# Block records by plain loads on SyncE, and a small block's second product as four strips of 192 outputs

## The chip, the cores and the metric

The kernel runs on one core of one Trainium2 chip. The metric is the device time of one execution in microseconds (us); lower is better. Times of the kernel before are the median of three runs. Beside them one execution was profiled; it has its own time, and a span, from the first to the last instruction of the program.

## The reference

Sigmoid attention over 8 batches, 12 heads, 448 positions and a head size of 64 gives 3584 rows of 768 numbers. Each row then goes through a mixture of experts with a skip: a row whose skip score is not positive stays as it is, another goes through the one expert, out of eight, that its gate logits choose.

```python
scores = scale * np.matmul(q, k.transpose(0, 1, 3, 2)) - np.log(S)
attn = 1.0 / (1.0 + np.exp(-scores))
x = (attn @ v).transpose(0, 2, 1, 3).reshape(3584, 768)
do_compute = x @ w_skip > 0
e_idx = np.argmax(xc @ w_gate, axis=1)          # xc = x[do_compute]
h = np.maximum(xc[mask] @ w1[e], 0.0)           # 768 -> 1024
y[mask] = gate_w[mask, None] * (h @ w2[e])      # 1024 -> 768
out[do_compute] = xc + y
```

## The kernel before

The first part (to about 284 us) is the attention, over 48 pairs of heads; meanwhile each row is given its expert, and a record (gate weight, row number) is scattered into `lst`, a table in device memory with a stretch of rows for each expert. From 284 to 324 us two blocks of 128 rows of the most used expert are computed. Meanwhile VectorE works out the list of the remaining blocks: from per-expert sums (`gt`, 17 columns) and one-hot masks over 64 list places (`m_f`, `m_a`, `m_p`), small matmuls into `ptab` make two things. One is `rix`, for each of the 64 places a column of 128 row numbers of `lst`: VectorE forms the first row of each place (`row`, L1072 to L1074) and a matmul with `ones_f` spreads it over 128 partitions (L1077). The other is `slots`, three rows of numbers for each place (L1081): whether the weights of another expert are to be loaded, of which, and the kind of the block.

From 324 us a loop (L1537) runs over the remaining 14 blocks. All engines run the same loop: each reads the kind of the block from `slots` into a register (a TENSOR_LOAD, L1089), branches (L1526, L1527, L1532) and runs one of four arms:

- FULL and SPLIT (`block`): 128 rows with weights that were split into a high and a low part (`wh1`, `wl1`, `wh2`, `wl2`), three products for each. SPLIT also makes the split weights of the next expert from the raw ones.
- HALF (`half`): up to 64 rows, with raw weights (`raw1`, `raw2`).
- FEW (`few`), the small block: up to 32 rows, with raw weights. TensorE's columns work as four groups of 32. In the first product (L1391, `ph`) each group makes 128 hidden numbers at a time. In the second (L1391, `py`) group g makes 384 outputs over one half of the eight chunks of h; so two groups hold partial sums of the same outputs. ScalarE scales two of them into `yt` (L1444), and VectorE adds the other two, scaled (L1446).

In FEW and HALF, SyncE issues the eight loads of the next expert's raw weights, 768 KB each: four of w1 after the first product (L1213), four of w2 after the second (L1222), on SyncE's one queue.

Rows and records are fetched ahead. During a block, `fetch` on GpSimd copies the row numbers out of `rn` (the record after next, L1267), issues an indirect DMA for the rows `xn` (L564), and another for the next record `rn` from `lst` by a column of `rix` (L1115); the ops on `jk`, `rn` and `rx` (L1266, L1268, L1269) stand before it as waits. `shift` on VectorE (L1283) moves `rix` by one column each block, through `riv`. `take_rec` (L1322) takes the record at the next block. `put` on GpSimd copies the row numbers (L1287, L1288), waits for the two halves of `yt` (L1293), copies them into `ys` (L1302) and issues the scatter that adds them to `out` (L574).

The order of instructions on each engine is written by hand (`manual_schedule`), in the order of the program's text; a framework adds the semaphores. After the last iteration the program ends when the last scatter has landed.

## Time and profile before

| | us |
|---|---|
| median of three runs | 526.61 (526.55 to 526.98) |
| the profiled execution's own time | 526.53 |
| its span | 524.8 |
| granted TensorE clock | 0.995 |
| TensorE matmul busy | 508.7 (97%) |
| VectorE, ScalarE, GpSimd busy | 296.1, 281.0, 262.5 |
| attention, first two blocks, loop (from the chain of waits) | to 284, to 324, to the end |

In the span's last 200 us the fourteen blocks of the loop follow one another; five of them are FEW, at 403.8, 428.9, 454.3, 480.3 and 507.2 us, and the last one ends the program. The profile counts an engine as busy when it computes; branches, register loads and the issue of DMAs belong to the engine's sequencer, which is listed apart (PEq, SPq and so on). The chain of waits is followed back from the last instruction: each piece is either work or what released it.

### The profile page before, as it was taken

To read this page: it belongs to the slowest core of one execution; us is meant where nothing else is said; L and a number is where in the kernel's file an instruction comes from. 1 tells how busy PE (TensorE), PEld (TensorE's weight loads), DVE (VectorE), ACT (ScalarE), POOL (GpSimd) and SP (SyncE) were. 2 spreads that over 40 slices of the span, in tenths; PEclk is the share of its full clock that TensorE was granted. 3 is DMA by queue.
4 is the path that set the end of the run, shared out by engine and by line. 5 is a ranking of instruction groups with operands and counts; after the bars stand their busy time and mean duration, and the time that the engine had idled before them with its cause. 6 is when DMAs were issued, how large, how long until landed. Compare 5 with 4: busy or idle time off the path is not lost.

```text
span 524.8 us, 15310 instructions
## 1 busy us (share of the span) xinstructions
PE 508.7 (97%) x5033; PEld 339.2 (65%) x5034; DVE 296.1 (56%) x721; ACT 281.0 (54%) x485; POOL 262.5 (50%) x414
## 2 busy tenths in 40 slices
PE   8999999999999999999989999999999999999991
PEld 7765555545545456555445989948669797978790
DVE  4556757648667676687684962862222322269422
ACT  5776776767767668677664211942112323268322
POOL 4523553443557666766574332553333645455644
PEclk9999999999999999999999999999999999999997
DMA  8999787898999999999955023979393959695942
GB/s 211 209 257 200 150 187 156 178 175 173 195 206 234 220 203 221 196 204 213 199 105 114 11 92 105 389 210 347 99 364 119 317 230 310 240 328 227 346 184 47
DMA packets 140288, 107.21 MB, mean 204 GB/s; under 512 B 97099, under 2 KB 112731, under 8 KB 140240
## 3 DMA queue, kind: packets, MB, share of 16 engines
q1 hardware_dynamic: 134000, 97.66, 70.0%
q0 software_dynamic: 4576, 8.65, 6.9%
q8 instruction: 30, 0.49, 0.4%
q10 hardware_dynamic: 1664, 0.26, 0.3%
q14 instruction: 18, 0.15, 0.1%
HBM read 98.49 MB, written 17.56 MB: 221 GB/s over the span
## 4 chain that ended last, share of the span: by engine, by line
PE 89%; DVE 3%; SPq 2%; DMA 2%; issue 1%; ACT 1%; POOL 0%; POOLq 0%; ACTq 0%; DVEq 0%
PE s L212 23%; PE pa L240 21%; PE ph L516 11%; PE py L544 11%; PE b_ph L516 3%; PE b_py L544 3%; PE ph L1391 3%; PE py L1458 2%; PE ph L1458 2%; PE pxt L492 2%; PE py L1391 2%; PE pl L280 1%; PE pht L530 1%; DMA out_dram<-y 1%; SPq L263 1%
## 5 line engine op out<-in xcount | busy, mean ns | idle before, releaser
L232 ACT ACTIVATE at<-s,bias 128x896 f32<-128x896 f32 (+1 forms) x191 | 173.3, 913 | 82.1 <-PE s L212 71.2
L212 PE MATMUL s<-x 64*64 64x448 f32 (+1 forms) x1528 | 165.4, 498 | 1.3 <-DVE wh L485 0.9
L240 PE MATMUL pa<-at,v 64*64 64x448 f32 (+1 forms) x1536 | 163.0, 489 | 0.0
L176 POOL COPY kq<-kq 32x896 f32<-32x896 f32 (+1 forms) x96 | 88.1, 917 | 94.6 <-DMA kq<-in_q_dram 59.0
L212 PEld LDWEIGHTS s<-x 64*64 64x64 f32 x1528 | 80.0, 191 | 53.1 <-issue 28.6
L240 PEld LDWEIGHTS pa<-at,v 64*64 64x64 f32 x1536 | 62.5, 133 | 54.9 <-issue 47.8
L194 DVE STREAM_TRANSPOSE x<-kq 128x448 f32<-128x448 f32 x94 | 80.8, 934 | 5.0 <-POOL kq L176 5.0
L250 DVE TENSOR_TENSOR xt<-xt,pa 128x448 f32<-128x448 f32 x48 | 29.7, 620 | 54.4 <-ACT xt L673 49.6
L414 POOL DMA_INDIRECT lst<-rec,idx x32 | 31.7, 989 | 17.4 <-DVE xt L250 5.8
L486 POOL TENSOR_TENSOR wl<-wr,wh 128x384 fp32r<-128x384 f32 (+1 forms) x28 | 31.2, 1125 | 12.6 <-DVE wh L485 8.1
L255 DVE STREAM_TRANSPOSE y<-xt 128x448 f32<-128x448 f32 x48 | 31.0, 645 | 6.8 <-DMA out_dram<-y 5.2
L574 POOL DMA_INDIRECT out_dram<-ys,rp x15 | 23.7, 1580 | 16.6 <-issue 8.4
L525 ACT ACTIVATE hs<-ph 128x512 f32<-128x512 f32 x14 | 8.3, 596 | 43.9 <-PE ph L516 37.5
L536 DVE TENSOR_TENSOR hl<-pht,hh 128x512 fp32r<-128x512 f32 x14 | 9.7, 690 | 36.5 <-ACT hh L535 22.8
L544 PE MATMUL py<-wh,hh 128*128 128x384 f32 x112 | 29.8, 347 | 0.0
L502 DVE TENSOR_TENSOR xl<-pxt,xh 128x384 fp32r<-128x384 f32 x30 | 15.3, 552 | 25.3 <-ACT xf L1097 17.8
L544 PE MATMUL py<-wh,hl 128*128 128x384 f32 x112 | 28.8, 338 | 0.0
L544 PE MATMUL py<-wl,hh 128*128 128x384 f32 x112 | 28.7, 337 | 0.0
L516 PE MATMUL ph<-wh,xh 128*128 128x512 f32 x84 | 25.7, 402 | 1.1 <-ACT yt L1444 0.8
L516 PE MATMUL ph<-wl,xh 128*128 128x512 f32 x84 | 26.6, 403 | 0.0
L673 ACT ACTIVATE xt<-pa 128x448 f32<-128x448 f32 x48 | 25.7, 536 | 0.8 <-PE pa L240 0.8
L516 PE MATMUL ph<-wh,xl 128*128 128x512 f32 x84 | 24.5, 395 | 0.0
(277 smaller groups left out, 686.4 us busy)
## 6 DMA issues: line engine op xcount, KB each, us to landing
raw<-in_moe_w_dram SPq DMA_DIRECT2D x64, 768.0 KB
v<-in_v_dram SPq DMA_DIRECT2D x48, 256.0 KB
out_dram<-y SPq DMA_DIRECT2D x192, 56.0 KB
kq<-in_k_dram SPq DMA_DIRECT2D x46, 224.0 KB
kq<-in_q_dram SPq DMA_DIRECT2D x46, 224.0 KB
wr<-in_moe_w_dram SPq DMA_DIRECT2D x12, 256.0 KB
wr<-in_moe_w_dram SPq DMA_DIRECT2D x16, 192.0 KB
lst<-fill SPq DMA_DIRECT2D x4, 464.0 KB
```

The source lines that it names most:

```text
L176: nc.gpsimd.tensor_copy(a[BT:, :, :, :BT], a[:BT, :, :, BT:])
L194: nc.vector.transpose(xs[:, n].rearrange("p (r j) -> p j r", j=NJ), t.rearrange("p (j d) -> p j d", d=D)[:, :, :BT],)
L212: nc.tensor.matmul(sc[m * D : (m + 1) * D, j, : qs.stop - qs.start], xs[r, 0, first::NR7], xs[r, 1, qs], start=True, stop=True,)
L232: nc.scalar.activation(at[:, :, :n], sc[:, :, :n], AF.Sigmoid, bias=bias, scale=SCALE)
L240: nc.tensor.matmul(pa[j * D : (j + 1) * D, r, qs], vt[rs, j, r + c if c < 3 else 3 * (1 - r), :], at[rs, j, : qs.stop - qs.start], start=( ...
L250: nc.vector.tensor_tensor(x, x, pa[:, 1, :S], op=ALU.add)
L255: nc.vector.transpose(y, xts[b][:, hp, :])
L414: put = nc.gpsimd.indirect_dma_start(out=lst[:, :], out_offset=bass.IndirectOffsetOnAxis(ap=idx[:, c : c + 1], axis=0), in_=rec[:, c, :], ...
L486: nc.gpsimd.tensor_tensor(lo, r, hi, op=ALU.subtract)
L516: nc.tensor.matmul(ph[h], a[:, j * P : (j + 1) * P], w[j][h], start=(n == 0), stop=(n == len(t) - 1),)
L544: last = nc.tensor.matmul(half_y(py, o), a[h][:, js], w[j][:, o * H2 : (o + 1) * H2], start=(j == 0 and n == 0), stop=(j == NK2 - 1 and n ...
L1391: nc.tensor.matmul(dst[g * SM : (g + 1) * SM, :n], a, w, start=(j == 0), stop=(j == most - 1), tile_position=(0, g * SM),)
```

## The change

Two things are changed together. First, the records come by plain DMAs issued by SyncE. `slots` gets a fourth row, ROW, the first row in `lst` of each place's block; SyncE reads it into a register and loads 128 consecutive rows of `lst`. `rix`, `ones_f`, the three ops on `row`, the matmul L1077, `shift`, `riv`, `rx` and the waits for them in `fetch` go. Second, in FEW's second product each of the four groups makes a strip of 192 outputs over all eight chunks of h. No partial sums are left to add: ScalarE scales two strips into `yt`, VectorE the other two.

```diff
-    V.tensor_scalar(row, m_f, f_rf, None, op0=ALU.mult)
-    V.scalar_tensor_tensor(row, m_a, f_ra, row, op0=ALU.mult, op1=ALU.add)
-    V.scalar_tensor_tensor(row, m_p, f_rp, row, op0=ALU.mult, op1=ALU.add)
-
     gemm1(1, range(3), xh0, xl0, ph)
-    nc.tensor.matmul(ptab[:, :NS], ones_f, row, start=True, stop=True)
-
-    HAS, NXT, TYP = range(3)
-    for n, (j, m) in enumerate(((2, m_a), (7, m_p), (12, m_f))):
+
+    ROW, HAS, NXT, TYP = range(4)
+    for n, (j, m) in enumerate(((1, m_a), (6, m_p), (11, m_f))):
         nc.tensor.matmul(
...
-    V.tensor_scalar(rix, ptab[:, :NS], slot_q, None, op0=ALU.add)
-    slots = const.tile([3, NS], I32, name="slots")
+    slots = const.tile([4, NS], I32, name="slots")
...
-    def gather_rec(dst, idx):
-
-        nc.gpsimd.indirect_dma_start(
...
+    def load_rec(dst, col):
+        row = entry(ROW, col, SP, NE * CAP - P)
+        nc.sync.dma_start(dst, lst[ds(row, P), :])
 
     for j in range(2):
-        gather_rec(recs[:, j, :], rix[:, j + 2 : j + 3])
-    gather_rec(rn, rix[:, 4:5])
+        load_rec(recs[:, j, :], slice(j + 2, j + 3))
+    load_rec(rn, slice(4, 5))
...
-    skip(4616 - DM)
+    skip(4688 - DM)
...
-    def fetch():
+    def fetch(i):
 
         pool.tensor_tensor(xn[:, 0:1], xn[:, 0:1], zf, op=ALU.add)
-        pool.tensor_tensor(jk, rn[:, 0:2], rn[:, 0:2], op=ALU.add)
         pool.tensor_copy(ri, rn[:, 1:2])
-        pool.tensor_tensor(rn[:, 0:1], rn[:, 0:1], zf, op=ALU.add)
-        pool.tensor_tensor(rx, rix[:, 5:6], zero, op=ALU.add)
         pool.tensor_tensor(rp[1], ri, zero, op=ALU.add)
         pool.tensor_tensor(rq, rp[1], zero, op=ALU.add)
         got = gather(xn, rp[1])
...
-        gather_rec(rn, rx)
+        load_rec(rn, ds(i + 5, 1))
...
         ready_x()
-        shift(dve)
 
-        for n, j in enumerate((0, 2, 1, 3)):
+        Q2 = DM // 4
+        for n, m in enumerate((0, 2, 4, 6, 1, 3, 5, 7)):
             for g in range(4):
-                o, h = g // 2, g % 2
-                m = j + h * (NK2 // 2)
                 quarter(
-                    py[h],
+                    py[g // 2],
                     g,
-                    H2,
-                    ht4[:, j % 2, 2 * h + j // 2, :],
-                    raw2[m][:, o * H2 : (o + 1) * H2],
+                    Q2,
+                    ht4[:, m % 2, m // 2, :],
+                    raw2[m][:, g * Q2 : (g + 1) * Q2],
                     n,
-                    NK2 // 2,
+                    NK2,
                 )
         for g in range(4):
             load_w2(g, nx)
-        for m in range(2):
-            for o in range(2):
...
+        for g in range(4):
+            s = slice(g * Q2, (g + 1) * Q2)
+            p = py[g // 2][g * SM : (g + 1) * SM, :Q2]
+            if g < 2:
+                nc.scalar.activation(yt[:SM, s], p, AF.Copy, scale=recs[:SM, 0, 0:1])
+            else:
+                weigh_sum(yt[:SM, s], p, recs[:SM, 0, 0:1])
```

## The prediction

> **What bounds the kernel now.** I read the busy shares first, then the shares of the chain of waits, then the chain through the loop, then the sequencer's own instructions.

> ```profile
> PE 508.7 (97%) x5033; PEld 339.2 (65%) x5034; DVE 296.1 (56%) x721; ACT 281.0 (54%) x485; POOL 262.5 (50%) x414
> ...
> PE 89%; DVE 3%; SPq 2%; DMA 2%; issue 1%; ACT 1%; POOL 0%; POOLq 0%; ACTq 0%; DVEq 0%
> ```

> TensorE (PE) is busy for 97% of the span and is 89% of the chain. So an edit counts only where it changes what PE executes, or makes PE stand, or lies behind PE's last instruction. VectorE (DVE) and GpSimd (POOL) are busy for about half the time: work taken from them in mid-loop is worth nothing by itself. The next rows are the chain through one small block (FEW at 428.87) into the FULL block behind it (start, duration, engine, tile, line).

> ```profile
> 428.87 2.81 PE ph L1391 x96
> 431.69 0.26 PE pht L1412
> ...
> 432.71 2.75 PE py L1391 x32
> 435.47 0.28 issue
> 435.75 6.53 PE ph L516 x27
> ```

> The first product is 96 matmuls in 2.81 us, the second 32 in 2.75 us, and at 435.47 PE stands for 0.28 us in "issue", which is no engine and no transfer: PE's sequencer was not yet through with the branch to the next arm. That small gap is where the change can hurt, so I read the four ends of FEW blocks that have a block behind them.

> ```profile
> 410.34 6.49 PE ph L516 x27
> 488.70 6.49 PE ph L516 x27
> 461.75 0.47 PE L516 MATMUL ph<-wh,xh 128*128 128x512 f32 x1 [0.80 <-ACT yt L1444]
> ```

> ```profile
> L1537 PEldq COMPARE_BRANCH  x1: 239/239/239, 408.5 to 408.5; - x1
> L1537 PEldq COMPARE_BRANCH  x1: 237/237/237, 433.7 to 433.7; - x1
> L1537 PEldq COMPARE_BRANCH  x1: 239/239/239, 459.1 to 459.1; - x1
> L1537 PEldq COMPARE_BRANCH  x1: 237/237/237, 486.5 to 486.5; - x1
> L1089 PEldq TENSOR_LOAD <-slots x1: 459/459/459, 409.1 to 409.1; - x1
> L1089 PEldq TENSOR_LOAD <-slots x1: 972/972/972, 434.3 to 434.3; - x1
> L1089 PEldq TENSOR_LOAD <-slots x1: 1265/1265/1265, 459.7 to 459.7; - x1
> L1089 PEldq TENSOR_LOAD <-slots x1: 446/446/446, 487.1 to 487.1; - x1
> L1089 PEldq TENSOR_LOAD <-slots x13: 302/308/1265, 340.0 to 505.0; - x13
> L1412 PEldq FUSED_REGOPS  x1: 42/42/42, 430.9 to 430.9; - x1
> ```

> The loop's branch (L1537) runs on PE's sequencer while PE still has matmuls queued. It starts at 408.5, 433.7, 459.1 and 486.5; the products end at 410.34 and 488.70 (the next block follows at once), 435.47, and 461.75 - 0.80 = 460.95. So the sequencer's lead is 1.84, 1.77, 1.85 and 2.2 us. From the branch to the next block's first matmul it needs 2.05 us at 433.7 (to 435.75) and 2.65 us at 459.1 (to 461.75); at the other two at most its lead. Much of that is the read of the block's kind: 0.459, 0.972, 1.265 and 0.446 us behind a FEW, where the fastest of 13 took 0.302 and the median 0.308. So the stalls now are 0, 0.28, 0.80 and 0: 1.08 us.

> **The change part by part.** The sum is made against the profiled execution, 526.53 us with a span of 524.8, 0.08 below the median of 526.61.

> *Prologue.* The matmul that spread the row numbers goes; it lies on the chain:

> ```profile
> 309.29 0.40 PE ptab L1077 x2
> ```

> That is -0.4. Its neighbours are PE as well, so nothing takes its place; bounds -0.8 (if the products behind it were held by the shorter VectorE chain too) to 0 (if the later `slots` holds PE instead). The first records now come by SyncE, in front of the first w1 load on its queue, and not by three gathers on POOL: POOL's gather form costs about 1 us of POOL each (0.99 at L1115, below), so they should land no later. I cost it at nothing.

> *FEW's products.* Each of five FEW blocks makes 16 quadruples of 192 columns for 8 of 384. The rows above hold two sizes of the same form: 96 matmuls are 24 quadruples of 128 in 2.81 us, 117 ns each; 32 are 8 of 384 in 2.75 us, 344 ns each. The line through both gives 0.885 ns a column and 174 ns at 192: 16 are 2.78 us, +0.03 a block, +0.1 in all (bounds 0 and +0.5, the latter with a fixed cost three times as large).

> *The end of FEW.* This is the main cost. I take PE's queue to hold a number of instructions, not a time, and the second product becomes 64 matmuls of 2.78 / 64 = 43 ns in place of 32 of 86 ns. Now the branch at 433.7 has 1.77 us or 20 matmuls of 86 ns in front of it, fewer than the 27 found next, so the queue is not full there; with 64 matmuls it would be. How far ahead is the sequencer then? At 430.9 PE's sequencer ran the register operation behind the first product's last matmul (L1412), and that product ended at 431.68: 0.78 us, or 27 matmuls of 2.81 / 96 = 29 ns, each with its weight load, were outstanding. 27 matmuls of 43 ns are 1.17 us; the branch comes a few instructions behind the last matmul, for which I allow 0.12 (three of the 42 ns of that operation): the branch is 1.05 us ahead of the product's end, against 1.77 to 2.2 now. The stall is then the time from branch to first matmul less 1.05. With the reads as recorded the first and the last end need the 2.05 of the second with their own read in place of its, 2.05 - 0.97 + 0.46 = 1.54 and 1.53, so the stalls are 0.49 and 0.48; the second 2.05 - 1.05 = 1.00; the third 2.65 - 1.05 = 1.60. In all 3.57, which is 2.5 more than before. With every read at 0.302 the path is 1.38 (2.05 - 0.97 + 0.30), three times 0.33, and at the SPLIT (2.65 - 1.265 + 0.302 = 1.69) 0.64: 1.63, +0.55 more than before. Which read is right I can't see: they were slow only behind a FEW, when a busy stretch of DMA begins, and that stays about as it was, but no row shows the cause. I take +1.1, nearer the faster end because 9 of the 13 reads were fast and the reads now fall later against the start of the w2 loads.

> [...]

> *The tail.* The last block is a FEW; nothing runs behind its scatter, and the chain after its product is short enough to read (start, duration, engine, line):

> ```profile
> 514.00 1.17 ACT L1444 ACTIVATE yt<-py,recs 32x384 f32<-32x384 f32 x2 [0.73 <-DVE xl L502]
> 514.83 1.26 DVE L1446 SCALAR_TENSOR_TENSOR yt<-py,recs,yt 32x384 f32<-32x384 f32 x2
> 515.11 0.99 POOL L1115 DMA_INDIRECT rn<-lst,rx  x1 [0.31 <-issue]
> 516.12 0.20 POOL L1287 TENSOR_TENSOR rp<-rid,zero 128x1 int32<-128x1 int32 x1
> 516.54 0.18 POOL L1293 TENSOR_TENSOR jk<-yt 32x2 f32<-32x2 f32 x1
> ...
> 518.65 1.41 POOL L574 DMA_INDIRECT out_dram<-ys,rp  x1 [0.62 <-issue]
> ```

> ```profile
> 514.00:515.00 1.00, 0.00 (x0) 0.00 (x0) 0.86 (x4) 0.97 (x2) 0.80 (x1) 1.00 0.81 154
> 515.00:515.50 0.50, 0.00 (x0) 0.00 (x0) 0.47 (x2) 0.17 (x1) 0.39 (x1) 1.00 0.03 0
> ```

> ```profile
> L1446 DVE SCALAR_TENSOR_TENSOR yt<-py,recs,yt 32x384 f32<-32x384 f32 x10 | 6.1, 613 | 0.7 <-ACT yt L1444 0.4
> L1444 ACT ACTIVATE yt<-py,recs 32x384 f32<-32x384 f32 x10 | 5.7, 574 | 4.4 <-DVE xl L502 2.2 <-DVE riv L1283 1.3 <-PE py L1391 0.7
> L1408 ACT ACTIVATE hs<-ph 128x128 f32<-128x128 f32 x10 | 2.8, 278 | 33.5 <-PE ph L1391 31.9 <-PE pxt L492 1.7
> ```

> Now the two halves pass ScalarE and then VectorE and end at 516.09; POOL is behind the record's gather until 516.10, so the two are equally late, and POOL's put starts at 516.12. Both go. POOL's gather of `rn` (0.99, and 0.31 of issue) is gone, so POOL could start put near 514.8, but put's first copy also waits for the scatter before it: the DMA rows show 154 GB/s until 515 and nothing after, so 515.05. The strips: 192 columns on ScalarE, by the line through 128 (278 ns) and 384 (574), are 352 ns; two are 0.70. VectorE's two (384 take 613) are about 0.76, beside ScalarE's and behind nothing. From the product's end at about 514.0 `yt` is whole at about 514.9, plus the small queue effect of a later start. So put is set by 515.05, 1.07 before 516.12, and what follows (518.65 and the landing) moves with it: -1.0. Bounds: -1.7 (if the wait for the previous scatter isn't the limit and put follows `yt`), 0 (if a later product end and POOL's other work give all of it back).

> *Records in mid-loop.* The record of the block after next now goes through SyncE's queue, behind the w1 loads that a FEW has just issued. The rows are stretches of the second block's time: length, then busy time of PE, PE's loads, VectorE, ScalarE, POOL, clock, DMA share, GB/s.

> ```profile
> 433.00:436.00 3.00, 2.72 (x33) 1.28 (x26) 0.98 (x3) 2.13 (x10) 2.19 (x9) 1.00 0.63 163
> 436.00:439.00 3.00, 3.00 (x14) 2.41 (x14) 1.94 (x9) 0.82 (x2) 1.43 (x2) 1.00 1.04 258
> 439.00:446.00 7.00, 7.00 (x38) 5.86 (x37) 0.92 (x3) 1.79 (x3) 4.03 (x14) 1.00 1.04 395
> ```

> ```profile
> 444.09 0.16 DVE L1322 COPY recs<-rn 128x2 f32<-128x2 f32 x1
> 447.76 0.69 DVE L536 TENSOR_TENSOR hl<-pht,hh 128x512 fp32r<-128x512 f32 x1 [3.51 <-issue]
> 470.06 0.16 DVE L1322 COPY recs<-rn 128x2 f32<-128x2 f32 x1
> 470.13 3.90 DVE L1234 TENSOR_TENSOR wl<-raw,wh 128x512 fp32r<-128x512 f32 x6
> ```

> Four w1 loads are 3.1 MB: 0.49 and 0.77 by 439, the remaining 1.9 MB at 395 GB/s until about 444. The record then lands at about 445, VectorE takes it at 444.09 now, and its next work of weight is at 447.76, after 3.5 us of idleness: hidden. At the SPLIT it is tighter: the same pace from 454.3 puts the record at 470 to 472, it is taken at 470.06, and VectorE has 3.9 us of `wl` right behind, on which the next products of PE hang. 0 to +0.8; I take 0, since in VectorE's order only that copy and what stands behind it slips, and PE at that time is in products of older weights for several us.

> [...]

> The sum: -0.4 + 0.1 + 1.1 - 1.0 = -0.2, 526.3 for the profiled execution and 526.4 with the 0.08 to the median. No change that can be seen.

> **The rivals.**
> 1. Slower: the slow reads stay as recorded, 0.46 to 1.27 us behind each FEW. Then the third term is +2.5 and the time 526.4 + 1.4 = 527.8. For it: all four reads behind a FEW were slow in this trace; against: they differ by a factor of three from one another, so an earlier or later one may fall anywhere. It decides slower from about 2.4 us of added stalls.
> 2. Faster: the queue holds five matmuls more (if the operation at 430.9 itself came 0.15 us, five of 29 ns, behind the last issue) and the reads are fast. Leads are then 1.05 + 5 x 0.043 = 1.27 or, without the allowance, 1.39; stalls at 1.39 are 3 x 0 + (1.69 - 1.39) = 0.3, so -0.8 in place of +1.1: 526.4 - 1.9 = 524.5; with the second read as recorded, 0.67 more: 525.2. For it: nine of thirteen reads were fast. Against: it needs both.
> 3. Slower: the records are late where VectorE or POOL waits for them. At the SPLIT +0.8 and at the FULL blocks' fetches, whose SyncE part may come behind its waits for the eight weight loads, up to 2.3: 527.2 to 528.7. Against: the 3.5 us of idleness at 444.
> 4. The tail gives nothing, as put waits for something that I don't see: 527.4, no difference.

> **How the numbers follow.** My forecast has a chance of 0.42, rival 1 0.22, rival 2 0.20, rival 3 0.06, rival 4 0.10. A measurement here can tell 0.2%, 1.05 us, from no change: faster means below 525.56, slower above 527.66. Rival 2 and a little of my own case (a tail gain of 1.7) are faster, 0.22; rivals 1 and 3 are slower, 0.28; the rest is 0.50. The range goes from 525.2, between my case and rival 2, to 528.0, just past rival 1; my own case alone spans 525.7 to 527.4.

> **What would show it.** In the profile of the changed kernel: no `ptab` product of 0.40 at 309; `py` of FEW at 64 matmuls in 2.75 to 2.85 us; PE's branch (L1537's counterpart) about 1.05 us before the end of the product, and stalls of 0.3 to 0.7 us in the chain's "issue" rows at three or four ends; the last scatter issued at about 3.6 us behind the last product's end, not 4.65; `take_rec` without a long wait at FULL blocks. The prediction is wrong if the leads are still 1.8 us (the queue isn't counted in instructions), if PE waits for `hl` in the SPLIT, or if the last scatter isn't 1 us earlier.

## The result and the profile after

The changed kernel takes 551.1 us (median of five runs, 550.25 to 552.32) against 526.98 of the kernel before: a ratio of 1.047, 95% interval 1.0457 to 1.0484. The forecast was 526.4 with a range to 528.0; the profiled execution of the changed kernel has 550.82 us, a span of 549.1 and a granted clock of 0.975 instead of 0.995.

The first view is of the changed kernel: from its page the busy shares, the granted clock in 40 slices and one group of instructions, and from its list of VectorE's groups one more (busy time, mean ns; idle time of the engine just before them, and what ended it).

```profile
PE 514.1 (94%) x5191; PEld 347.2 (63%) x5192; DVE 290.2 (53%) x688; ACT 279.9 (51%) x485; POOL 236.5 (43%) x355
...
PEclk9999999999999999999999999999999898988986
...
L541 PE MATMUL py<-wh,hl 128*128 128x384 f32 x112 | 32.2, 371 | 16.4 <-DVE hl L533 16.4
...
L1293 DVE COPY recs<-rn 128x2 f32<-128x2 f32 x14 | 3.6, 255 | 54.3 <-SPq L1524 44.3 <-issue 9.9
```

TensorE now waits 16.4 us in the second product of the big blocks for `hl`, which VectorE makes, and VectorE had stood 44.3 us in front of `take_rec` (L1293 here, L1322 before). A wait on the record has come up through VectorE's order. From the first matmul of each block in the two traces (us):

| stretch | before | after | difference |
|---|---|---|---|
| start to the first block of the loop | 323.55 | 322.93 | -0.6 |
| to the first FEW | 80.16 | 79.75 | -0.4 |
| the blocks behind a FEW: FULL, FULL, SPLIT, FULL | 18.53, 18.51, 18.52, 18.54 | 23.62, 23.46, 27.37, 23.42 | +23.8 |
| four FEW with a block behind | 29.36 | 28.70 | -0.7 |
| last FEW to its product's end | 6.63 | 6.66 | 0 |
| from there to the end | 11.01 | 13.20 | +2.2 |

Four blocks hold the loss. (The -0.7 is no gain of the strips: in the kernel before, the fourth FEW took 8.36 us with short waits for ScalarE, and in the changed kernel it stands behind a SPLIT that is 8.9 us longer and takes 7.24.) The timeline of the first of the four, SyncE's issues first, then VectorE, and then TensorE's waits in all four:

```profile
405.09 3.45 SPq L1194 DMA_DIRECT2D raw<-in_moe_w_dram  x4
410.29 0.01 SPq L1105 DMA_DIRECT2D rn<-lst  x1
410.52 4.14 SPq L1203 DMA_DIRECT2D raw<-in_moe_w_dram  x4
427.47 0.35 SPq L1105 DMA_DIRECT2D rn<-lst  x1
```

```profile
427.18 0.17 DVE L1293 COPY recs<-rn 128x2 f32<-128x2 f32 x1 [9.19 <-SPq L1524]
427.29 0.69 DVE L533 TENSOR_TENSOR hl<-pht,hh 128x512 fp32r<-128x512 f32 x1
```

```profile
428.04 0.62 PE L541 MATMUL py<-wh,hl 128*128 128x384 f32 x2 [3.43 <-DVE hl L533]
...
458.64 0.62 PE L541 MATMUL py<-wh,hl 128*128 128x384 f32 x2 [3.31 <-DVE hl L533]
...
492.85 1.01 PE L541 MATMUL py<-wh,hl 128*128 128x384 f32 x2 [6.13 <-DVE hl L533]
523.99 0.62 PE L541 MATMUL py<-wh,hl 128*128 128x384 f32 x2 [3.24 <-DVE hl L533]
```

The record that `take_rec` needs was issued at 410.29, behind w1 and ahead of w2. VectorE goes on only at 427.18, and TensorE, which had other products for a while, stands 3.43 us. The windows of that block say what happened at 427 (columns as in the prediction: clock, DMA share and GB/s last):

```profile
418.00:424.00 6.00, 6.00 (x39) 5.83 (x38) 0.00 (x0) 2.66 (x10) 1.50 (x2) 1.00 1.04 394
424.00:428.00 4.00, 0.61 (x4) 0.29 (x2) 0.82 (x3) 0.00 (x0) 0.57 (x3) 1.00 0.50 197
428.00:429.00 1.00, 0.96 (x5) 0.96 (x6) 0.91 (x2) 0.00 (x0) 0.36 (x1) 1.00 0.09 8
429.00:433.00 4.00, 4.00 (x16) 4.00 (x15) 0.00 (x0) 0.00 (x0) 1.09 (x3) 0.57 0.29 98
```

The weights stop moving at 427: VectorE went on when the last w2 load had landed, not when the record had. The last row is a second loss behind the first. One microsecond after TensorE resumed, its granted clock fell to 0.57 for four microseconds, 4 x 0.43 = 1.7 us. So this block loses 3.43 + 1.7 = 5.1 us. The SPLIT loses 6.13 and 2.7 more: 0.3 in a shorter wait of the same kind, and 2.3 by the clock, which stands at half from 490.54 to 497.37, while TensorE resumes at 492.85. The four together lose 23.8.

The semaphores give the reason. The trace records which semaphore, a counter, each transfer raises, and which ones an instruction waits for (141 to 148 there, 0 to 7 here): in the first of the four blocks w2's last load raises 0 sixteen times, from 425.93 to 426.99 us, and `take_rec` waits there for 0 and then for 4, until 427.01 and 427.08 us. SyncE's transfers take these eight in turn. In a small block w1's four loads have 0 to 3, the record 4, and w2's four loads 5, 6, 7 and 0 again; in a FULL or SPLIT block, which loads only a record, that record has 0. A reader of `rn` doesn't know which kind of block came before, so `take_rec` waits for both 0 and 4. In this block the record's last raise of semaphore 4 is at 418.58 us, 0.6 us after VectorE had come free; the last raise of semaphore 0 by w2 is at 426.99, and VectorE's wait for 0 ends behind it. The row names SyncE (L1524) because SyncE itself stands at the branch for semaphore 0, and sets its count for the readers at 427.02.

So semaphore 0 is complete at 426.99 us, when the ninth transfer, w2's last 768 KB, has landed. Before the change the records came through GpSimd's own semaphores, and the eight weight loads had one each: in the small block at 428.87 of that trace the record, issued at 436.75 us, raises 134, and the loads, issued from 433.08 to 440.35, raise 141 to 148. In the changed kernel the readers wait for the later transfer, and the price of sharing is time, 16.4 us of TensorE's waits.

### The profile page after: what moved, and what is told of

It is laid out like the page before. It is cut to its first block, busy times and chain, and to the rows that moved or that the text cites. A ratio compares the mean times of both kernels' runs of the same rounds, so it can differ in the third digit from the quotient of the medians.

```text
span 549.1 us, 15708 instructions
## 1 busy us (share of the span) xinstructions
PE 514.1 (94%) x5191; PEld 347.2 (63%) x5192; DVE 290.2 (53%) x688; ACT 279.9 (51%) x485; POOL 236.5 (43%) x355
## 5 line engine op out<-in xcount | busy, mean ns | idle before, releaser
L541 PE MATMUL py<-wh,hl 128*128 128x384 f32 x112 | 32.2, 371 | 16.4 <-DVE hl L533 16.4
L541 PEld LDWEIGHTS py<-wh,hl 128*128 128x128 f32 x112 | 22.3, 209 | 18.1 <-DVE hl L533 18.0
L541 PE MATMUL py<-wh,hh 128*128 128x384 f32 x112 | 32.3, 372 | 0.0
L1293 DVE COPY recs<-rn 128x2 f32<-128x2 f32 x14 | 3.6, 255 | 54.3 <-SPq L1524 44.3
L541 PE MATMUL py<-wl,hh 128*128 128x384 f32 x112 | 30.9, 359 | 0.0
L1376 ACT ACTIVATE hs<-ph 128x128 f32<-128x128 f32 x10 | 2.8, 278 | 48.6 <-PE ph L1359 47.5
```

The source lines that it names most:

```text
L541: last = nc.tensor.matmul(half_y(py, o), a[h][:, js], w[j][:, o * H2 : (o + 1) * H2], start=(j == 0 and n == 0), stop=(j == NK2 - 1 and n ...
```

## The experiments

Theory A is that explanation (A1 in the expectations). Theory B is the one the prediction had as its third rival: the record itself is late, because it stands behind 3.1 MB of w1 in SyncE's ring.

**One part at a time.** The kernel before with the strips alone:

```diff
 # before.py: few() only
-        for n, j in enumerate((0, 2, 1, 3)):   # 8 groups of 384, partial sums
+        for n, m in enumerate((0, 2, 4, 6, 1, 3, 5, 7)):   # 16 groups of 192
```

> The kernel before with only the second part of the change: strips of 192, records still gathered by GpSimd. Theory A (all of the loss comes from the records) expects no long wait of TensorE: the four branch stalls as in the changed kernel, 1.9 us in all in place of 1.1 (+0.85), the five products within 0.1, the tail up to 1.0 shorter: 525.7 to 527.5 us, clock 0.995. Theory S (the strips themselves bring the waits, through later yt or PSUM) expects 545 to 551.

Measured: 528.73 us, ratio 1.0025 (1.0011 to 1.0039). The records alone (the changed kernel with few()'s old second product):

> The changed kernel with the second product of small blocks as before (8 quadruples of 384, partial sums added): the records part alone. Theory A expects the four blocks behind a small block to lose 5, 5, 9 and 5 us as in the changed kernel and the tail 2 to 3: 549 to 551 us, clock about 0.975. Theory S expects 526 to 527.

Measured: 547.01 us, ratio 1.0386 (1.0357 to 1.0414). Three of the waits for `hl` are 3.2 to 6.3 us; in the last FULL block it is 2.56, and there the clock stayed at 1.00. So the records bring the loss, and the strips cost 0.25%, 1.3 us. The time lies below the 549 to 551 expected: that last block takes 21.21 us for the changed kernel's 23.42, and the end of the program 10.70 for 13.20.

**Fewer bytes in the last load.** The fourth w2 load leaves out its second chunk.

```diff
-            load_w2(g, nx)
+            load_w2(g, nx, 1 if g == 3 else 2)   # chunks in the load
```

> The changed kernel with the fourth load of w2 cut to one of its two chunks (384 KB less, so the output is not the reference's): still nine transfers in a small block, and the last one lands 384 KB / 395 GB/s = 1.0 us earlier. Theory A1 (the record's readers wait for the fourth w2 load) expects each of TensorE's waits for hl to shrink by 1.0 us, from 3.4 to 3.6 to about 2.5 and at the SPLIT block from 6.7 to 5.7; 541 to 548 us, the lower end if the half clock behind the waits goes too. Theory B (the record itself is late behind w1) expects no difference: 550 to 552.

Measured: 545.16 us. The waits of the same four blocks, from its timeline:

```profile
427.11 0.61 PE L541 MATMUL py<-wh,hl 128*128 128x384 f32 x2 [2.49 <-DVE hl L533]
456.58 0.62 PE L541 MATMUL py<-wh,hl 128*128 128x384 f32 x2 [2.34 <-DVE hl L533]
...
488.44 1.01 PE L541 MATMUL py<-wh,hl 128*128 128x384 f32 x2 [5.05 <-DVE hl L533]
...
518.49 0.61 PE L541 MATMUL py<-wh,hl 128*128 128x384 f32 x2 [2.27 <-DVE hl L533]
```

3.43, 3.31, 6.13 and 3.24 became 2.49, 2.34, 5.05 and 2.27: 0.94 to 1.08 less each, where 1.0 was expected. The bytes that count are those of the last w2 load, issued after the record. Theory B alone is out.

**The record earlier.**

```diff
+        next_row(i)             # copy of the row numbers, then the record's load
         for h in range(2):
             for g in range(2):
                 load_w1(g, h, nx)
```

> The changed kernel with the record's load issued ahead of w1's four loads in small and half blocks, still nine transfers; GpSimd's copy of the row numbers is moved up with it. The record lands about 6 us earlier. Theory A1 expects the waits to stay, since the last w2 load still shares a semaphore with it: 548 to 553 us. Theory B expects them to go: 523.5 to 526.

Measured: 569.0 us, ratio 1.0794. With nothing of w1 ahead of it the record has semaphore 0 in every block, still shared with the last w2 load, and w1 and w2 now go later (w1 5.8 us behind the first matmul of a small block, for 2.4): the waits for `hl` are 27.9 us in six blocks. The waits stay, as A expects; the time is 16 us above A's range, and that estimate did not have the later weights in it.

**A queue of its own, the same semaphores.** `nc.scalar.dma_start` in place of `nc.sync.dma_start` in `load_rec`:

> The changed kernel with the records loaded by ScalarE, so on a queue of their own, but on the same eight semaphores as SyncE's loads. Theory A1 expects long waits as before or longer, since ScalarE itself now waits for the weight loads: 550 to 590 us. Theory B (order in SyncE's ring) expects the waits to go: 524 to 527 us.

Measured: 558.45 us (one run). A ring of its own doesn't help. The waits look different, though: `hl` has only 0.6 us left, and TensorE stands 12.4 us before the small blocks' second product, 7.9 for `hh` and 2.4 for `ht`. The last two are ScalarE's own work, which now comes late behind its waits for the semaphores; what ends the 12.4 the profile doesn't name.

**Eight transfers.** The third and fourth w2 load as one of 1.5 MB:

```diff
-        for g in range(4):
+        for g in range(3):      # the third has four chunks
             load_w2(g, nx)
```

> The changed kernel with the third and fourth load of w2 as one of 1.5 MB: the same bytes on the same queue, but eight transfers of SyncE in a small block and not nine. Theory A1 (nine transfers take eight semaphores in turn, so that the last weight load has the semaphore that the record's readers wait for) expects no wait for the record: the four blocks get their 23.8 us back and the tail about 3, 523.5 to 525 us, clock 0.995. Theory B (the record stands in the ring behind w1 and comes too late itself) expects the loss to stay: 549 to 552.

Measured: 535.82 us, ratio 1.0171 (1.0147 to 1.0196). Its waits of TensorE (total, times, longest), and VectorE in the first FULL block behind a FEW:

```profile
PE ph L1420 <- DMA rn<-lst: 2.3, 1, 2.3
PE ph L513 <- issue: 1.6, 3, 0.9
...
PE py L541 <- DVE hl L533: 0.3, 1, 0.3
```

```profile
422.88 0.17 DVE L1293 COPY recs<-rn 128x2 f32<-128x2 f32 x1 [1.11 <-DMA rn<-lst]
```

The 16.4 us are 0.3, and the four blocks take 18.55, 18.40, 18.93 and 18.38 us: this part of A holds. The record's own landing is seen here: VectorE waits 1.11 us for it, hidden. But 8 us of loss are left where A expected a gain. Some 3 of them lie outside the program's span (time less span is 3.5 to 5.2 us, for 1.7 to 3.5 in the kernel before), and nothing in the trace explains them. Inside it the first row names a new wait: TensorE's first product of a half block waits for a record. It reads the w1 tile whose load has semaphore 0, and so has the FULL or SPLIT block's record: the record's last raise is at 344.85 us, and TensorE starts at 344.98. Sharing works in both directions, which I had not seen when I wrote that expectation. The same wait stays with eight transfers and the old second product, whichever two loads are made one:

> Records by SyncE, the third and fourth load of w2 as one (eight transfers), and the second product of small blocks as before the change. A1 expects no wait for records but the 2.2 us at the first half block that the eight-transfer kernel with strips showed; branch stalls near 0 as with the records part alone; against before -0.6 (prologue), -0.9 (FULL blocks 0.1 shorter each), -1.0 (branch stalls), +2.2 and +0.4: 525 to 528 us.

> As the former, but with two loads of w1 as one in place of w2's, so that the last transfer stays 768 KB. A1 expects no wait for records either; if the wait at the first half block came with the 1.5 MB at the end of the first weights, it is gone: 523.5 to 526 us; if it comes from the record standing behind 6 MB of first weights, it stays: 525 to 528.

Measured: 530.49 us (1.0083; 1.0055 to 1.0111) and 529.88 us (1.0074; 1.0048 to 1.01). In the second, TensorE waits for `rn` five times:

```profile
PE ph L1368 <- DMA rn<-lst: 2.3, 4, 1.3
PE ph L1434 <- DMA rn<-lst: 2.0, 1, 2.0
```

**No sharing.** Three ways to keep records and weights apart. First, eight transfers (two w1 loads as one) with the record the first of them, without and with the strips:

> Records by SyncE with eight transfers in a small block (two loads of w1 as one) and the record's load the first of them, so that it has the first semaphore in every kind of block and shares it with no weight load; second product as before the change. Theory A1, now in both directions (readers of a record wait for a weight load on its semaphore, readers of a weight tile wait for a record on theirs), expects the 2.2 us at the first half block and the 1.3 us in front of small blocks to go as well: 523.5 to 526 us; w1 is issued 1 to 2 us later, which may cost up to 1.5 at the SPLIT block. If these waits were for the record's own place in the ring, the 2.2 us at the first half block stays: 526 to 528.

> The same with the strips of 192: both parts of the change, without shared semaphores. Against the former the branch stalls +0.8 to +1.9 (lead 1.0 us) and the tail -0.9 to 0: 523.5 to 527.5 us. The prediction's own sum, 526.4, should hold here if only the shared semaphores made it wrong.

Measured: 527.9 us (1.0043; 1.0022 to 1.0064) and 532.1 us (1.0117; 1.0085 to 1.015). No wait for `rn` is left on TensorE. Without strips, the five FULL blocks and the first three FEW are 1.7 us shorter together than in the kernel before; the SPLIT block is 2.9 and the FEW behind it 0.9 longer. There w1 is issued later (9.9 us behind the first matmul of the FEW before it, for 4.6), which is the likely cause. With the strips, 3.2 to 5.2 us of the time lie outside the span again. Second, loads of 64 bytes that move the record to one place in the turn in every kind of block:

```diff
+        for j in range(pads):   # 3 with eight transfers, 4 with nine; FULL and SPLIT only
+            nc.sync.dma_start(pad[j][:1, :], lst[0:1, :])
         load_rec(rn, ds(i + 5, 1))
```

> Records by SyncE with eight transfers (two w1 loads as one), second product as before the change, and three loads of 64 bytes ahead of the record's load in FULL and SPLIT blocks, so that the record has the fourth semaphore in every kind of block. Theory A1 expects neither readers of records nor readers of w1 to wait for one another: against the eight-transfer kernel without these loads the 2.2 us at the first half block and the 1.3 us in front of two small blocks go: 523 to 525.5 us, below the kernel before. If the first of these waits is for the record's own place behind 6 MB of first weights, 525 to 527.5.

> The changed kernel, strips, nine transfers and order in the ring untouched, with only four loads of 64 bytes put ahead of the record's load in FULL and SPLIT blocks, so that the record has the fifth semaphore in every kind of block and the last w2 load shares with a 64-byte load alone. Theory A1 expects the four waits for hl to go and about 20 to 23 us to come back: 527 to 531 us. Theory B, and any theory in which nine transfers or the bytes ahead of the record matter by themselves, expects 549 to 552.

Measured: 529.18 us (1.0047; 1.0031 to 1.0063) and 540.87 us (1.0256; 1.023 to 1.0282), both above what A expected. In the first no wait for `rn` is left and the SPLIT is at 18.53 us, but four of the five small blocks take 8.0 to 8.2 us, for 6.8 to 7.2 without the 64-byte loads, which no listed wait accounts for in full. The second is the purest test: a small block's nine transfers and their order are untouched, and the records go in the same order. The waits for `hl` are gone and the four blocks take 18.37, 18.34, 18.36 and 19.75 us, but only about half of the loss comes back (1.026 for 1.047), since the 64-byte loads land behind w2 and share with w1:

```profile
PE ph L1362 <- DMA pad<-lst: 4.6, 4, 1.6
PE ph L513 <- ACT yt L1411: 2.3, 2, 1.3
PE ph L1362 <- SPq L1527: 1.3, 1, 1.3
```

Third, one 64-byte load ahead of w1 in small and half blocks, eight transfers in all, w1 in its old place ahead of the record:

> Records by SyncE, second product as before the change, two loads of w1 and two of w2 as one, and one load of 64 bytes ahead of w1 in small and half blocks, so eight transfers; the record of a FULL block shares a semaphore only with that 64-byte load, which lands before w1, and w1 is issued no later than in the kernel before. Theory A1 expects no wait for a shared semaphore anywhere and none of the loss at the SPLIT block that came with the later w1: against before -0.6 (prologue), -0.9 (FULL blocks), -1 to -2 (small blocks' ends), up to +2 where a 1.5 MB load lands later: 522.5 to 526 us. If the loss at the SPLIT block and the block behind it (3.9 us in the kernel with the record first) does not come from w1's later issue, it stays: 526 to 528.5.

> The same with the strips of 192, so both parts of the change without shared semaphores and with w1 in its old place. Theory A1 with the branch term of the strips as measured alone (+1.3 to +1.6 us against the kernel before) and a tail up to 1.0 shorter expects 523.5 to 527.5 us; if the prediction's sum (526.4) failed only by the shared semaphores, the time lies within 1.1 of it.

Measured: 530.74 us (1.0068; 1.0043 to 1.0092) and 533.57 us (1.0109; 1.0083 to 1.0135): both above what A expected. Without the strips the loss sits in the SPLIT block (23.44 us for 18.52):

```profile
475.39 0.17 DVE L1303 COPY recs<-rn 128x2 f32<-128x2 f32 x1 [3.82 <-DMA rn<-lst]
475.60 3.70 DVE L1225 TENSOR_TENSOR wl<-raw,wh 128x512 fp32r<-128x512 f32 x6
```

```profile
479.96 0.62 PE L541 MATMUL py<-wh,hl 128*128 128x384 f32 x2 [1.63 <-DVE hl L533]
```

Here it is the record's own place in the ring: it lands at 475.26, behind the last of w1 at 475.06, and the `wl` work stands behind `take_rec`; the clock then stands at half from 480.68 to 484.09. So theory B is true at this one place in this kernel. It isn't a cost of the place alone: w1 went out 6.7 us behind the first matmul of its block, for 4.6 before, because SyncE stood at the branch until 457.72, when the w2 load of 1.5 MB had landed. In the two kernels with 64-byte loads in FULL and SPLIT blocks the record stands behind all of w1 too, and the SPLIT takes 18.53 and 18.36 us. No version with the records on SyncE beats the kernel before.

**What was left over.** Records by GpSimd again, without the shift:

```diff
-        pool.tensor_tensor(rx, rix[:, 5:6], zero, op=ALU.add)
+        pool.tensor_tensor(rx, rix[:, ds(i + 5, 1)], zero, op=ALU.add)
```

> The kernel before with its gathers on GpSimd, but without the column shift on VectorE: fetch reads the column of rix at the loop's own index. In every kernel with records by SyncE the FULL blocks are 0.10 to 0.15 us shorter and the stalls behind small blocks mostly gone, and two things left together there, the shift and GpSimd's gather of rn. Theory V (the shift's copies are what slows FULL blocks) expects eight blocks 0.1 shorter and the small blocks' ends as before: 525.4 to 526.3 us at a before of 526.6. Theory G (the gather) expects no difference: within 0.3 of before.

Measured: 525.28 us against 525.18, ratio 1.0012 (0.9998 to 1.0027), the FULL blocks 18.54 to 18.56 as before. No cost of the shift can be seen. That the blocks are 0.1 us shorter wherever GpSimd's gather is gone speaks, by exclusion, for theory G, or for the small ops on GpSimd that went with the gather; neither was tested by itself.

## Why the prediction was wrong

**The step that failed is "Records in mid-loop"**, costed at 0 with an end of +0.8. It asked when the record lands, and answered about right: I put the landing some 9.5 us behind the small block's product (445 against 435.47); with eight transfers VectorE takes the record 422.88 - 413.03 = 9.85 us behind the product, and in the changed kernel itself it landed 418.58 - 409.29 = 9.3 us behind it. What failed is the step from "landed" to "hidden": it did not ask which other transfers complete the same semaphore. The kernel before has eight loads in a small block; with the record it is nine, over eight semaphores. So VectorE stood until the last w2 load was in, 8.4 us after the record, where the prediction let it go on with the record. The third rival named the right waiting engine, with a chance of 0.06 and a price of 0.8 to 2.3 us, and its remark on SyncE's waits for the eight weight loads comes nearest to what happened; the price is 23.8 us in four blocks, 16.4 of waits and 7.4 of the clock and small remainders. The prediction's own sign, PE waiting for `hl` in the SPLIT, came with 6.13 us.

**Prologue**, -0.4: not settled. The product of 0.40 us is gone and the loop starts 0.6 earlier in this trace, but over all the traces here it starts between 322.2 and 326.5 us, and the earliest is one that still has the product.

**FEW's products**, +0.1: right, 2.81 us each for 2.82.

**The end of FEW.** The lead was forecast at 1.05 us. The branches (start), and the reads of the block's kind, in the changed kernel:

```profile
L1498 PEldq COMPARE_BRANCH  x1: 244/244/244, 408.3 to 408.3; - x1
L1498 PEldq COMPARE_BRANCH  x1: 239/239/239, 439.0 to 439.0; - x1
L1498 PEldq COMPARE_BRANCH  x1: 239/239/239, 469.5 to 469.5; - x1
L1498 PEldq COMPARE_BRANCH  x1: 243/243/243, 504.3 to 504.3; - x1
L1079 PEldq TENSOR_LOAD <-slots x1: 314/314/314, 408.9 to 408.9; - x1
L1079 PEldq TENSOR_LOAD <-slots x1: 398/398/398, 439.6 to 439.6; - x1
L1079 PEldq TENSOR_LOAD <-slots x1: 353/353/353, 470.1 to 470.1; - x1
L1079 PEldq TENSOR_LOAD <-slots x1: 348/348/348, 505.0 to 505.0; - x1
```

The products end at 409.29, 439.95, 470.52 and 505.47: leads of about 1.0, 1.0, 1.0 and 1.1, for 1.8 to 2.2 before. The stalls are 0.39, 0.48, 0.70 and 0.36, 1.93 in all or +0.85 for a forecast of +1.1. With the strips alone the leads are the same and two reads were 0.57 and 0.96, so the stalls are 2.65, +1.6. So the lead that the prediction worked out from a fixed number of instructions came out, 1.0 to 1.1 us for 1.05, and the second rival's 1.27 or 1.39 is seen at no end. That the queue counts instructions was the estimate behind it; the runs show the leads alone. What stays open is why the reads differ. They were 0.31 to 0.32 with the records alone and 0.85 to 1.15 with eight transfers and the record first, both without GpSimd's gather, so the gather isn't the reason.

**The tail**, -1.0: mis-sized. From the product's end to the last scatter's issue it is 540.41 - 535.91 = 4.50 us for 4.85 (the prediction measured from 514.0, where the product ends at 513.80), -0.35. As forecast, put waits for the scatter before it, and that one landed later:

```profile
537.91 0.18 POOL L1258 TENSOR_TENSOR rp<-rid,zero 128x1 int32<-128x1 int32 x1 [1.24 <-DMA out_dram<-ys,rp]
...
540.41 1.38 POOL L571 DMA_INDIRECT out_dram<-ys,rp  x1 [0.61 <-issue]
```

From that issue to the end it is 8.7 us for 6.2; the strips alone have 6.2. The 2.5 us lie in the program's last steps, where the engines wait for one another. TensorE ends one of its waits there at 544.86 us and comes to its next instruction at 548.31, 3.45 us later; in the kernel before that takes 0.15 us (523.18 to 523.33). In between there is one transfer, 16 KB from 545.86 to 546.75 on queue 8, which the profile's page lists as "instruction". Five kernels here have such a transfer in these steps, and they need 8.7 to 9.6 us from the last scatter's issue to the end: the changed one, the ones with the shorter last load, with the record first and nine transfers, with ScalarE's queue, and with nine transfers and 64-byte loads. All the others need 6.0 to 6.2. That TensorE waits for this load is inferred from the times alone, and why it falls there in some kernels isn't known.

Had the semaphores been the only error, the kernel with both parts and none shared (533.57 us) would lie near 526.4. It doesn't. In its trace the span is 5.3 us longer than before, of which 3.2 are in the first four FEW blocks, 1.5 in the first SPLIT and the HALF behind it, 1.1 in the second SPLIT and 0.7 ahead of the loop, against 1.1 shorter elsewhere. Another 3.4 lie outside the span in the profiled execution, 0.2 to 3.5 in the others. The ends of the FEW blocks are the one of these terms that the prediction had, at +1.1; their stalls are 3.17 there, +2.1.

## What to carry to other kernels

Before a transfer is moved to another queue, count the transfers that this queue then has in one pass of the loop, and see which of them raise the same semaphore. Here the record's reader waited for the last of them (VectorE until 427.01 us, for a record that had landed at 418.58), and with eight transfers a reader of w1 waited for the record (TensorE until 344.98 us, behind a last raise at 344.85). Look for it in the wait lists, at the merge of branches above all, where one reader waits for every branch's semaphore. And price a wait of TensorE of about two to three microseconds at up to 1.7 us more than its length: here the clock stood at half for 3.4 us behind a wait of 3.43 us and behind one of 1.75, and stayed at full behind waits of 2.56, 2.34 and 2.27.

## What was not expected of the hardware

```profile
407.00:409.00 2.00, 0.83 (x5) 0.83 (x6) 1.69 (x4) 0.00 (x0) 0.79 (x4) 1.00 0.04 4
409.00:411.00 2.00, 2.00 (x8) 2.00 (x7) 0.04 (x1) 0.00 (x0) 1.21 (x3) 0.50 0.29 40
```

```profile
520.00:524.00 4.00, 1.44 (x8) 1.12 (x7) 1.45 (x4) 0.00 (x0) 0.57 (x3) 1.00 0.46 179
524.00:526.00 2.00, 2.00 (x14) 2.00 (x13) 0.28 (x1) 0.00 (x0) 1.45 (x3) 1.00 0.12 22
```

The moments at which the granted clock changes, which the traces record, say what decides. In the four blocks of the changed kernel it falls and rises at 429.10, 432.51, 459.82, 463.23, 490.54, 497.37, 524.67 and 528.09 us. All of these lie on one grid of 3.413 us: from 432.51 to 459.82 it is 8 steps, from 463.23 to 490.54 again 8. The other kernels have the same grid with another start; in the kernel before, the clock is at full from 7.16 to 519.16 us, 150 steps of 3.413. So here the idle time is counted by steps of the grid:

| wait of TensorE | its idle time in the steps it falls on | clock behind |
|---|---|---|
| 3.43 us, changed kernel | 1.08, 2.35 | half |
| 1.75 us, record first | 1.75 | half |
| 2.56 us, records alone | 0.83, 1.73 | full |
| 2.34 us, shorter last load | 1.00, 1.34 | full |
| 2.27 us, shorter last load | 0.46, 1.81 | full |

In all the traces, from 300 us on, a clock at full fell behind every step in which TensorE stood for 2.10 us or more (in the changed kernel behind 2.23, 2.35, 2.73 and 3.41), and behind none with 1.66 us or less. Between these, with about half of a step idle, it came both ways (fallen behind 1.72, 1.75 and 1.96, not fallen behind 1.73 to 1.98 in eight steps); the ends of matmuls are modelled in the profile, so the bound can't be read more closely from them.

So a step in which TensorE stood for part of the time could be enough: in the kernel with the record first, 1.75 us of waiting in a step of 3.413 us had the clock at 0.50 behind it.
